# Block transposes on VectorE for maxima and sums over keys, from the seventeenth attention unit on

## The chip, the cores and the metric

One Trainium2 chip, one core. The metric is the device time of one launch in microseconds, the median of the runs. Three runs of the kernel before took 1505.15, 1508.67 and 1516.34 us.

## The reference

Attention with pooled queries, then a feed-forward layer with a maximum over three products. Everything is float32.

```python
q, k, v: (8, 8, 1152, 64)          # batch, heads, sequence, head size
q_pool = q.reshape(B, H, S // 2, 2, D).mean(axis=3)          # 576 queries
scores = (1 / sqrt(64)) * q_pool @ k.T
scores = scores - max(scores, over keys)
attn = exp(scores); attn = attn / (sum(attn, over keys) + 1e-9)
x = (attn @ v) -> (4608, 512)      # tokens x (heads * head size)
h = maximum(maximum(x @ w1, x @ w2), x @ w3)                 # 512 -> 768
out = h @ w_out                                              # 768 -> 512
```

The maximum and the sum run over the 1152 keys of one query. In this kernel scores lie with keys on the partitions and queries along the free axis, so both run across partitions. That is the place of the change.

## The kernel before, in words

**Units.** Two heads (a pair) and half of their queries (288) make one unit of attention. There are 8 batches x 4 pairs x 2 halves = 64 units, `d` = 0 to 63; eight units make a batch. The feed-forward part (FFN) of batch b is offered to the planner when the first unit of batch b + 1 has been laid down; that of the last batch comes at the end.

**One unit.** For each of nine blocks of 128 keys TensorE makes scores `pqk` for both heads (L441, L442; keys and queries are kept as a high and a low part). ScalarE copies them to `s` (L447) and VectorE keeps a running maximum `acc` of 128 partitions x 2 heads x 288 queries (L453, L456). Then the maximum over the partitions, for each head: TensorE turns `acc` in three pieces of 96 queries (`rows`, L489, tile `pmt`), VectorE reduces them (`reduce`, L495, tile `m`), and TensorE turns the result back, repeated over all partitions (`bcast`, L502, tile `pmb`). VectorE subtracts `pmb` from `s` (L517), ScalarE takes exp (L523), GpSimd adds the nine blocks of keys to `ksum` (L536, L538), TensorE multiplies with the values (`pav`, L556), ScalarE copies that to `xr` (L565).

**The sum over keys.** For units 16 to 63 (`early` is false) TensorE multiplies `ksum` by a matrix of ones (`total`, L570), 64 columns wide for each head, so that the sum of every query stands on all partitions of its head; ScalarE adds eps (L574), VectorE takes the reciprocal of 128 x 288 (L577), GpSimd scales `xr` (L580). Units 0 to 15 go another way, which the change leaves alone: sums by one-column products (`columns`, L587), eps and reciprocal on six columns, a spread by TensorE (`spread`, L602).

**The FFN.** `xr` is split into a high and a low part (`xh`, L644; `xl`, L647). TensorE makes `ph` (L788), ScalarE and VectorE evacuate it with the maximum over the three weights (L806, L808), the result is split again (L816, L819), TensorE makes `po` (L844). Its weights are converted once, in the first FFN: 24 pieces, each with four instructions on VectorE (L697, L702, L707, L710); later FFNs fetch the converted weights with DMAs.

**What sets the order.** `arrange` is a list scheduler that runs before the program is built. Each step has its engine, a planned cost, the steps it comes after, and a rank (its unit's number plus a constant from the table `RANK`; the FFN's ranks also grow with their place in it). Whenever a planned engine is free it takes the ready step of lowest rank. The order found is the order in which each engine's instructions are issued; every engine works its list strictly in order. The planned costs, such as `pe(400)` for `rows`, only shape that order.

**PSUM.** `ps_a` and `ps_b` are one buffer each: `pmt`, `pmb` of head 0 live in the first, those of head 1 and the value product of later units in the second. `ps_ff` has two buffers for the FFN's products and the sums.

Of the kernel before, what the change touches and what calls it, by code (L numbers as in the profile page):

```python
# [18 lines left out]
P = 128  # L19
D = 64  # L20
NK = 9
NQ = 576
QH = 288
# [5 lines left out]
EPS = 1e-9  # L29
# [2 lines left out]


RANK = {
    "qk": -95.970825,
    "cp": 3.506714,
    "mx": -112.160269,
    "rows": -148.312644,
    "red": 23.466841,
    "bc": -142.276903,  # L40
    "sub": 99.862451,
    "exp": -189.653089,
    "keys": 148.893694,
    "av": 19.232023,
    "xcopy": -206.02547,
    "psum": 18.355097,
    "eps": -181.047585,
    "inv": 113.796689,
    "xm": -22.916262,
    "load": -43.210932,  # L50
    "prep": 250.679273,
    "move": 65.149737,
    "split": -97.511902,
    "ffn": -47.593054,
    "rate": 0.801853,
    "mm": 67.95383,
    "fetch": -234.19152,
    "evac": -68.37474,
    "hhigh": 38.661498,
    "hlow": -51.844784,  # L60
    "conv": 191.981971,
    "rate0": 3.325971,
    "first_qk": 41.083979,
    "first_cp": -105.959101,
    "first_mx": 56.619279,
    "first_sub": 16.712798,
    "first_exp": 260.515882,
    "first_keys": -71.869651,
    "first_av": -60.410117,
    "first_xcopy": 62.582893,  # L70
    "first_psum": -24.318635,
    "first_inv": -22.423915,
    "first_xm": -3.450351,
    "first_load": -260.256351,
    "first_prep": 57.308365,
    "first_move": -123.943607,
    "first_split": 239.216553,
}
LAG = {
    "act": {"act": 0.06, "pe": 0.27},  # L80
# [5 lines left out]
WINDOW = 4096 / 1200  # L86
BUSY = 3072
EARLY = 16
SPLIT = 8
WARM = 10  # L90
APART = 0
# [110 lines left out]
def pe(n):  # L202
    return ("pe", n * 1e-3)
# [6 lines left out]
def dve(n):  # L210
    return ("dve", 0.065 + n / 960)
# [7 lines left out]
def tile_attention_ffn(  # L219
# [9 lines left out]
    nc = tc.nc  # L229
    B = qT.shape[0]  # L230

    cpool = ctx.enter_context(tc.tile_pool(name="cpool", bufs=1))
# [5 lines left out]
    small = ctx.enter_context(tc.tile_pool(name="small", bufs=2))  # L238
# [5 lines left out]
    ps_ff = ctx.enter_context(tc.tile_pool(name="ps_ff", bufs=2, space=PSUM))  # L244
# [7 lines left out]
    eps = cpool.tile([P, 1], F32, name="eps")  # L252
    nc.vector.memset(eps, EPS)

    wo_hi = cpool.tile([P, 6, DM], F32R, name="wo_hi")
    wo_lo = cpool.tile([P, 6, DM], F32R, name="wo_lo")
# [10 lines left out]
    def step(key, at, engines, fn, after, **kw):  # L267
        return Step(plan, lambda: at + R[key] + (R.get("first_" + key, 0) if at < 8 else 0), engines, fn, after, **kw)
# [26 lines left out]
    qk, av, xout, splits, chain = {}, {}, {}, {}, {}  # L295
# [119 lines left out]


    units = {}
    uses, last, finish, scaled, spreads = [[], []], [None], {}, {}, {}

    def scores(d, n, half):  # L420
        o = units[d] = Job()
# [6 lines left out]
        for kk in range(NK):  # L428
            apart = d < APART and kk % 3 == 2
            for hs in [(0, 1), (1, 2)] if apart else [(0, 2)]:  # L430
# [48 lines left out]
                if not apart:  # L479
                    uses.append([c, x])  # L480

        o.rows, o.subs, o.exps, o.pt, o.pb, o.m = [], [[], []], {}, {}, {}, {}
        pools = (ps_a, ps_b)
        for h in range(2):

            def rows(e, h=h):
                o.pt[h] = pools[h].tile([P, 512], F32, tag="ab"[h], name=f"pmt{d}_{h}")
                for i in range(3):
                    nc.tensor.transpose(  # L489
                        o.pt[h][:96, i * P : (i + 1) * P], o.acc[:, h, 96 * i : 96 * i + 96], ident  # L490
                    )

            def reduce(e, h=h):
                o.m[h] = small.tile([96, 3], F32, tag=f"m{h}", name=f"m{d}_{h}")
                nc.vector.tensor_reduce(  # L495
                    o.m[h], o.pt[h][:96, : 3 * P].rearrange("p (t k) -> p t k", t=3), axis=AX.X, op=ALU.max
                )

            def bcast(e, h=h):
                o.pb[h] = pools[h].tile([P, 512], F32, tag="ab"[h], name=f"pmb{d}_{h}")  # L500
                for i in range(3):
                    nc.tensor.transpose(  # L502
                        o.pb[h][:, 96 * i : 96 * i + 96],
                        o.m[h][:, i : i + 1].broadcast_to([96, P]),
                        ident[:96, :96],
                    )
# [3 lines left out]
            o.rows.append(x)  # L510
            x = step("red", d, [("dve", 0.467)], reduce, [x])
            b = step("bc", d + 0.1 * h, [pe(335)], bcast, [x])
# [31 lines left out]
    def values(d, b, j):  # L544
# [19 lines left out]
        def x_copy(e):  # L564
            nc.scalar.copy(x, o.pav[:, :QH])  # L565

        def total(e):
            o.psm = ps_ff.tile([P, 512], F32, tag="ff", name=f"psum{d}")
            for h in range(2):
                nc.tensor.matmul(o.psm[64 * h : 64 * h + 64, :QH], ones, o.ksum[:, h], start=True, stop=True)  # L570

        def add_eps(e):
            o.rs = small.tile([P, QH], F32, tag="rs", name=f"rs{d}", bufs=1)
            nc.scalar.activation(o.rs, o.psm[:, :QH], AF.Identity, bias=eps)  # L574

        def reciprocal(e):
            nc.vector.reciprocal(o.rs, o.rs)  # L577

        def scale(e):
            vec[e].tensor_tensor(x, x, o.rs, op=ALU.mult)  # L580


        def columns(e):
            o.psm = ps_ff.tile([P, 512], F32, tag="ff", name=f"psum{d}")
# [68 lines left out]

        def rest(ready):

            t = chain[d] = step(
                "av" if ready else "psum",
                d + 0.99,
                [pe(486)],
                total,  # L660
                [o.sums[-1]] + ready,
                cols=1152,
                mode=1,
                take="ff",
            )
# [203 lines left out]
    d = n = 0  # L869
# [56 lines left out]
```

## Time and profile before

| | |
|---|---|
| median of three runs | 1508.67 us |
| profiled execution, span from first to last instruction | 1509.3 us |
| granted TensorE clock, mean | 0.963 |
| TensorE busy with products | 1437.4 us, 95% |
| TensorE busy with weight loads (beside the products) | 1234.1 us, 82% |
| VectorE | 1085.3 us, 72% |
| ScalarE | 912.7 us, 60% |
| GpSimd | 1133.2 us, 75% |
| first running maximum of unit 8 / 16 / 32 / 63 on VectorE | 165.6 / 328.3 / 737.2 / 1384.3 us |

In the tables of the profile PE is TensorE's products, PEld its weight loads, DVE VectorE, ACT ScalarE, POOL GpSimd. A group's row gives its line, engine, operation, output and inputs by the program's names, shapes and count, then busy us and the mean ns of one, then idle time in front of it with what ended it. A row in order of time gives start, length, engine and line, count. A row of the windows gives each engine's busy us in that stretch, the granted clock, the DMA engines' busy share and what they moved. The products of L556, L570 and L587 leave two records each, so four records of L570 are two products.

### The profile page before, as it was taken

The page shows a single profiled execution, that of the slowest core. Times are in us where ns is not written, and L with a number is a line of the kernel's source. Part 1 is how long each engine was busy: PE and PEld are TensorE (multiplying, and loading weights), DVE is VectorE, ACT ScalarE, POOL GpSimd, SP SyncE. Part 2 cuts the span into 40 slices and gives each one's busy share as a digit, 9 for nine tenths or more (in the row PEclk, how much of TensorE's full clock was granted, in tenths as well). Part 3 has the DMA queues.
Part 4 walks back from the last instruction along what each step waited for, and adds up shares of the span by engine and source line. Part 5 has one row for each costly group of instructions (what it writes and reads, how often), then busy time and mean ns, then how long its engine had stood idle before and what let it go on. Part 6 is the DMA issues. An engine that isn't in the chain of part 4 may idle for free.

```text
span 1509.3 us, 28532 instructions
## 1 busy us (share of the span) xinstructions
PE 1437.4 (95%) x10640; PEld 1234.1 (82%) x10640; DVE 1085.3 (72%) x1417; ACT 912.7 (60%) x1508; POOL 1133.2 (75%) x867
## 2 busy tenths in 40 slices
PE   7889898989679999999999999999999999999999
PEld 6566676777448999898988888888888988889899
DVE  4889789999897754676668776877578776877310
ACT  4766666775566644565666665776566665666311
POOL 1899899998988547667978787887888787885610
PEclk7878999999869999999999999999999999999999
DMA  6565455565544554456545654565555664562141
GB/s 185 145 176 157 111 166 155 162 197 174 173 112 116 171 165 159 132 163 178 162 139 166 194 183 110 164 192 152 153 150 157 189 189 122 164 178 84 61 163 64
DMA packets 105273, 231.51 MB, mean 153 GB/s; under 512 B 14384, under 2 KB 80816, under 8 KB 95920
## 3 DMA queue, kind: packets, MB, share of 16 engines
q1 hardware_dynamic: 104560, 229.11, 51.7%
q8 instruction: 85, 1.39, 0.4%
q10 hardware_dynamic: 576, 0.59, 0.2%
q14 instruction: 52, 0.43, 0.1%
HBM read 135.27 MB, written 18.87 MB: 102 GB/s over the span
## 4 chain that ended last, share of the span: by engine, by line
PE 66%; POOL 2%; DVE 2%; DMA 1%; issue 1%; ACT 1%; SPq 0%; ACTq 0%; POOLq 0%; DVEq 0%
PE ph L788 26%; PE pav L556 12%; PE po L844 10%; PE pqk L441 7%; PE pqk L442 7%; PE pmt L489 2%; PE psum L570 2%; PE pmb L502 1%; POOL ksum L538 1%; DMA qq<-qraw 1%; POOL xl L647 0%; DVE acc L456 0%; ACT s L447 0%; DMA kraw<-in_kT_dram 0%; DVE w L702 0%
## 5 line engine op out<-in xcount | busy, mean ns | idle before, releaser
L538 POOL TENSOR_TENSOR ksum<-ksum,s 128x576 f32<-128x576 f32 x448 | 650.5, 1452 | 29.6 <-ACT s L523 6.6
L788 PE MATMUL ph<-xh,w 128*128 128x288 f32 x2304 | 532.1, 300 | 11.1 <-DVE hm L808 10.2
L447 ACT COPY s<-pqk 128x576 f32<-128x576 f32 x576 | 361.3, 638 | 127.1 <-PE pqk L442 116.1
L517 DVE TENSOR_TENSOR s<-s,pmb 128x864 f32<-128x864 f32 x384 | 394.4, 1045 | 37.4 <-PE pmb L502 37.3
L788 PEld LDWEIGHTS ph<-xh,w 128*128 128x128 f32 x2304 | 392.7, 189 | 20.4 <-DVE hm L808 12.3
L441 PE MATMUL pqk<-qq,kc 128*128 128x288 f32 x1152 | 358.1, 326 | 40.0 <-DVE acc L456 30.6
L456 DVE TENSOR_TENSOR acc<-acc,pqk 128x576 f32<-128x576 f32 x448 | 334.8, 747 | 85.0 <-ACT s L447 81.7
L523 ACT ACTIVATE s<-s 128x864 f32<-128x864 f32 x384 | 354.4, 929 | 56.7 <-DVE s L517 53.0
L788 PE MATMUL ph<-xl,w 128*128 128x288 f32 x1152 | 341.2, 296 | 0.0
L442 PE MATMUL pqk<-qq,kc 128*128 128x288 f32 x1152 | 333.9, 304 | 0.0
L556 PE MATMUL pav<-s,v 128*64 128x288 f32 x2304 | 308.4, 422 | 0.0
L441 PEld LDWEIGHTS pqk<-qq,kc 128*128 128x128 f32 x1152 | 226.3, 196 | 74.7 <-DVE acc L456 47.1
L556 PEld LDWEIGHTS pav<-s,v 128*64 128x64 f32 x2304 | 167.4, 142 | 120.3 <-issue 17.0
L442 PEld LDWEIGHTS pqk<-qq,kc 128*128 128x128 f32 x1152 | 228.5, 198 | 0.0
L788 PEld LDWEIGHTS ph<-xl,w 128*128 128x128 f32 x1152 | 218.0, 189 | 0.0
L536 POOL TENSOR_TENSOR ksum<-s 128x576 f32<-128x576 f32 x64 | 91.7, 1433 | 105.0 <-ACT s L523 101.3
L819 POOL TENSOR_TENSOR h_lo<-hm,h_hi 128x288 fp32r<-128x288 f32 x96 | 79.1, 827 | 100.4 <-ACT h_hi L816 100.4
L495 DVE TENSOR_REDUCE m<-pmt 96x3 f32<-96x384 f32 x128 | 69.5, 550 | 108.8 <-PE pmt L489 108.6
L808 DVE TENSOR_TENSOR hm<-hm,ph 128x288 f32<-128x288 f32 x192 | 86.1, 449 | 79.0 <-PE ph L788 77.5
L577 DVE RECIPROCAL rs<-rs 128x288 f32<-128x288 f32 (+1 forms) x64 | 96.3, 1505 | 56.5 <-ACT rs L574 54.7
L337 POOL TENSOR_TENSOR kraw<-kraw 128x1152 fp32r<-128x1152 f32 x31 | 83.0, 2678 | 51.3 <-DMA qraw<-in_qT_dram 25.8
L844 PE MATMUL po<-h_hi,wo_hi 128*128 128x288 f32 x384 | 115.9, 302 | 0.0
(55 smaller groups left out, 1467.8 us busy)
## 6 DMA issues: line engine op xcount, KB each, us to landing
w<-w_split SPq DMA_DIRECT2D x63, 1024.0 KB, 5.2
kc<-kraw SPq DMA_DIRECT2D x384, 96.0 KB, 2.3
qq<-qraw SPq DMA_DIRECT2D x252, 144.0 KB, 2.9
v<-in_vr_dram SPq DMA_DIRECT2D x32, 576.0 KB, 3.8
kraw<-in_kT_dram SPq DMA_DIRECT2D x31, 576.0 KB, 4.6
qraw<-in_qT_dram SPq DMA_DIRECT2D x31, 576.0 KB, 4.3
w<-in_win_dram SPq DMA_DIRECT2D x18, 512.0 KB, 6.1
w_split<-w SPq DMA_DIRECT2D x9, 1024.0 KB, 5.0
```

What stands on the lines that cost most here:

```text
L441: nc.tensor.matmul(ps[:, h - hs[0], :QH], w, qq[:, 0, h], start=True, stop=False)
L442: nc.tensor.matmul(ps[:, h - hs[0], :QH], w, qq[:, 1, h], start=False, stop=True)
L447: nc.scalar.copy(o.s[kk // 3][:, kk % 3, slice(*hs)], o.ps[kk, hs][:, :, :QH])
L456: nc.vector.tensor_tensor(acc, acc, ps, op=ALU.max)
L517: nc.vector.tensor_tensor(s, s, o.pb[h][:, None, :QH].broadcast_to([P, 3, QH]), op=ALU.subtract)
L523: nc.scalar.activation(s, s, AF.Exp, scale=SCALE)
L536: vec[e].tensor_tensor(o.ksum, o.s[0][:, 0], x, op=ALU.add)
L538: vec[e].tensor_tensor(o.ksum, o.ksum, x, op=ALU.add)
L556: nc.tensor.matmul(o.pav[64 * h : 64 * h + 64, :QH], pr.v[:, kk, h], o.s[kk // 3][:, kk % 3, h], start=(kk == 0), stop=(kk == NK - 1),)
L577: nc.vector.reciprocal(o.rs, o.rs)
L788: nc.tensor.matmul(t.ps[:, :QH], w[:, a, kk], xx[:, kk, qs], start=(kk == 0 and i == 0), stop=(kk == 3 and i == 2),)
L844: nc.tensor.matmul(t.ps[:, :QH], ww[:, kk, ms], hh[:, kk, qs], start=(kk == 0 and i == 0), stop=(kk == 5 and i == 2),)
```

## The change

From unit 16 on (`TURN = 16`):

- **Maxima.** VectorE reduces every 32 x 32 block of `acc` over the partitions of that block (`blocks`, L501: a reduction that transposes its input by blocks), which leaves 18 columns, in a tile of 72 columns whose rest is zero. TensorE turns this tile once (`turn`, L511). VectorE takes the maximum over the four groups of partitions (`groups`, L515), copies it three times beside itself (`repeat`, L524), TensorE turns it back (`turn_back`, L530), and VectorE spreads it by two block transposes of a broadcast column (`spread_max`, L540), one for each head, into `pmb`.
- **Sums.** VectorE sums every 32 x 32 block of `ksum` in the same way (`block_sums`, L648). TensorE adds the four groups with a matrix `fold` (`fold_sums`, L660), nine columns for each head instead of 288. VectorE adds eps (L666), takes the reciprocal of nine columns (L669) and spreads it by one block transpose (`spread_sums`, L674). ScalarE's addition of eps is gone.
- **Set-up.** `fold` is made from the identity (L258), two tiles are cleared (L266), `eps` is gone.
- **Order.** All constants of `RANK` are new, and with them the place of every step in each engine's list.

Units 0 to 15 keep their steps. The lines above are those of the changed kernel.

```diff
 RANK = {
-    "qk": -95.970825,
+    "qk": -992.300111,
...
+TURN = 16
+ROWS = 72
+BLOCK = 32
...
+        def blocks(e):
+            nc.vector.tensor_reduce(
+                tp[:, : 2 * QH // BLOCK],
+                o.acc.rearrange("p h (b i) -> p (h b) i", i=BLOCK),
+                axis=AX.X,
+                op=ALU.max,
+                apply_transpose=True,
+            )
+
+        def turn(e):
+            o.pb[0] = pools[0].tile([P, 512], F32, tag="a", name=f"pmb{d}_0")
+            nc.tensor.transpose(o.pb[0][:ROWS, 384:512], tp, ident)
+
+        def groups(e):
+            o.m = small.tile([ROWS, P], F32, tag="m", name=f"m{d}")
+            nc.vector.tensor_reduce(
+                o.m[:, :BLOCK],
+                o.pb[0][:ROWS, 384:512].rearrange("b (g i) -> b i g", i=BLOCK),
+                axis=AX.X,
+                op=ALU.max,
+            )
...
+        def turn_back(e):
+            nc.tensor.transpose(o.pb[0][:, 288 : 288 + ROWS], o.m, ident[:ROWS, :ROWS])
+
+        def spread_max(e, h):
+            if h:
+                o.pb[1] = pools[1].tile([P, 512], F32, tag="b", name=f"pmb{d}_1")
+            n = QH // BLOCK
+            nc.vector.transpose(
+                o.pb[h][:, :QH].rearrange("p (b i) -> p b i", i=BLOCK),
+                o.pb[0][:, 288 + n * h : 288 + n * (h + 1), None].broadcast_to([P, n, BLOCK]),
+            )
...
-            x = step("rows", d + 0.1 * h, [pe(400)], rows, [tops[-1], gone] + (old.subs[h] if old else []))
...
+            if d < TURN:
+                x = step("rows", d + 0.1 * h, [pe(400)], rows, [tops[-1], gone] + (old.subs[h] if old else []))
...
+                    x = step("red", d, [dve(2 * QH)], blocks, [tops[-1]])
+                    x = step("rows", d, [pe(150)], turn, [x] + old.subs[0] + old.spreads)
+                    x = step("red", d, [dve(P)], groups, [x])
+                    x = step("red", d, [("dve", 0.17)], repeat, [x])
+                    turned = step("bc", d, [pe(150)], turn_back, [x])
+                b = step("spread", d + 0.1 * h, [dve(QH)], lambda e, h=h: spread_max(e, h), [turned, gone] + old.subs[h])
...
-            t = chain[d] = step("av" if ready else "psum", d + 0.99, [pe(486)], total, [o.sums[-1]] + ready, ...)
-            e1 = step("eps", d, [("act", 0.395)], add_eps, [t, scaled.get(d - 1)], give="ff")
-            t = step("inv", d, [("dve", 1.87)], reciprocal, [e1])
+            t = chain[d] = step("inv", d, [dve(2 * QH)], block_sums, [o.sums[-1], folded.get(d - 2)])
+            t = folded[d] = step("av" if ready else "psum", d + 0.99, [pe(260)], fold_sums, [t] + ready, ...)
+            t = step("inv", d, [("dve", 0.15)], add_eps9, [t, spreads.get(d - 2)], give="ff")
+            t = step("inv", d, [("dve", 0.18)], reciprocal9, [t])
+            t = spreads[d] = step("inv", d, [dve(QH)], spread_sums, [t, scaled.get(d - 1)])
```

Three places of the order. First TensorE in a late unit, around the value product. Before, the key sum (`psum`, two products) stands ahead of the value product (`pav`), then come transpositions (`pmt`) and broadcasts (`pmb`) among the next unit's score products (`pqk`) and FFN products (`ph`):

```order
L570 MATMUL psum_9883<-ksum_9536,ones 64x288 x2
L556 MATMUL pav_9890<-s_0_9465,v_9183 64x288 x6
L556 MATMUL pav_9890<-s_1_9516,v_9183 64x288 x6
L556 MATMUL pav_9890<-s_2_9579,v_9183 64x288 x6
L489 MATMUL pmt_0_9921<-ident,acc_9760 96x128 x3
L441 MATMUL pqk_0_9927<-qq_0_9611,kc_0_9541 128x288
...
L489 MATMUL pmt_1_9935<-ident,acc_9760 96x128 x3
...
L502 MATMUL pmb_0_9948<-ident,m_0_9933 128x96 x3
...
L502 MATMUL pmb_1_9961<-ident,m_1_9945 128x96 x3
```

Now, at the corresponding place:

```order
L455 MATMUL pqk_1_9652<-qq_0_9390,kc_0_9242 128x288
L511 MATMUL pmb_0_9658<-ident,tops_105 72x128
L660 MATMUL psum_9660<-ks_9541,fold 64x9 x2
L628 MATMUL pav_9665<-s_0_9234,v_8956 64x288 x6
L628 MATMUL pav_9665<-s_1_9292,v_8956 64x288 x6
L628 MATMUL pav_9665<-s_2_9354,v_8956 64x288 x6
L530 MATMUL pmb_0_9658<-ident,m_9663 128x72
L932 MATMUL po_2_0_9647<-h_hi_8007,wo_hi 128x288
```

Twelve transpositions of a unit became one turn (L511) and one turn back (L530), and the key sum has nine columns. In this unit the value product stands between the two turns; in most units it is FFN and score products.

Second VectorE in the same place. Before, from the last running maximum (L456) to the first subtractions (L517):

```order
L456 TENSOR_TENSOR acc_9760<-acc_9760,pqk_8_9877 128x576
L577 RECIPROCAL rs_9910<-rs_9910 128x288
L495 TENSOR_REDUCE m_0_9933<-pmt_0_9921 96x3
L495 TENSOR_REDUCE m_1_9945<-pmt_1_9935 96x3
L517 TENSOR_TENSOR s_0_9725<-s_0_9725,pmb_0_9948 128x3x288
```

Now:

```order
L469 TENSOR_TENSOR acc_9463<-acc_9463,pqk_8_9602 128x576
L501 TENSOR_REDUCE tops_105<-acc_9463 128x18
L515 TENSOR_REDUCE m_9663<-pmb_0_9658 72x32
L524 COPY m_9663<-m_9663 72x96
L666 TENSOR_SCALAR rc_9687<-psum_9660 128x9
L669 RECIPROCAL rc_9687<-rc_9687 128x9
L674 STREAM_TRANSPOSE rs_9690<-rc_9687 128x288
L540 STREAM_TRANSPOSE pmb_0_9658<-pmb_0_9658 128x288
L540 STREAM_TRANSPOSE pmb_1_9711<-pmb_0_9658 128x288
L589 TENSOR_TENSOR s_0_9445<-s_0_9445,pmb_0_9658 128x3x288
```

VectorE has eight instructions between the last maximum and the first subtraction where it had three. The sum's block reduction (L648) stands elsewhere, among the running maxima.

Third TensorE at the start of unit 24 (its first `pqk_0`), with the FFN product that stands ahead of it; in `ph_f_j_c` f counts the six column blocks of the FFN, j the three weights, c the half of the tokens. Before:

```order
L788 MATMUL ph_0_1_0_4916<-xh,w_0_3736 128x288 x2
L788 MATMUL ph_0_1_0_4916<-xl,w_0_3736 128x288
L788 MATMUL ph_0_1_0_4916<-xh,w_0_3736 128x288
L441 MATMUL pqk_0_4933<-qq_0_4701,kc_0_4552 128x288
L442 MATMUL pqk_0_4933<-qq_0_4701,kc_0_4552 128x288
```

Now:

```order
L876 MATMUL ph_4_2_1_5287<-xh,w_7_5070 128x288
L876 MATMUL ph_4_2_1_5287<-xl,w_7_5070 128x288
L876 MATMUL ph_4_2_1_5287<-xh,w_7_5070 128x288
L454 MATMUL pqk_0_5292<-qq_0_5052,kc_0_4940 128x288
L455 MATMUL pqk_0_5292<-qq_0_5052,kc_0_4940 128x288
```

When unit 24 begins, the FFN of the second batch stood in its first column block and now stands in its fifth. Counted over the whole list, the FFN products ahead of units 16, 20 and 24 were 276, 432 and 609 and are 399, 627 and 927, of 4608 in all.

More of the change, by code (lines that the diff above doesn't have):

```diff
@@ L34 @@
 RANK = {
-    "qk": -95.970825,
[L36 to L77, printed above, removed]
+    "qk": -992.300111,
+    "cp": 412.643831,
+    "mx": -1545.58781,
+    "rows": -759.1027,
+    "red": -325.246265,
+    "bc": -393.499534,
+    "sub": 2521.190112,
+    "spread": 51.107148,
+    "exp": -1655.988307,
+    "keys": 270.561796,
+    "av": -222.863284,
+    "xcopy": -2706.766959,
+    "psum": 75.873898,
+    "inv": -402.42614,
+    "xm": -2720.80782,
+    "load": 1943.234015,
+    "prep": -435.679461,
+    "move": 73.350202,
+    "split": 2454.226534,
+    "ffn": -1042.838197,
+    "rate": 227.744589,
+    "mm": 2028.536726,
+    "fetch": -804.9704,
+    "evac": 96.686784,
+    "hhigh": 2166.527179,
+    "hlow": -315.242909,
+    "conv": 505.137841,
+    "rate0": 5.466173,
+    "first_qk": 799.041515,
+    "first_cp": -875.506095,
+    "first_mx": -3464.107417,
+    "first_sub": 1648.535981,
+    "first_exp": 1378.011731,
+    "first_keys": -1207.515197,
+    "first_av": 986.355502,
+    "first_xcopy": -999.302149,
+    "first_psum": -259.061214,
+    "first_inv": 793.255621,
+    "first_xm": 2071.499672,
+    "first_load": 345.70598,
+    "first_prep": -968.961452,
+    "first_move": 286.644876,
+    "first_split": -867.421677,
 }
@@ L251, in tile_attention_ffn @@
     nc.vector.memset(ones, 1.0)
-    eps = cpool.tile([P, 1], F32, name="eps")
-    nc.vector.memset(eps, EPS)
+    fold = cpool.tile([P, D], F32, name="fold")
+    for i in range(D // BLOCK):
+        nc.vector.tensor_reduce(
+            fold[:, BLOCK * i : BLOCK * (i + 1)],
+            ident.rearrange("p (g i) -> p i g", i=BLOCK),
+            axis=AX.X,
+            op=ALU.add,
+        )
+    tops_ = [cpool.tile([P, ROWS], F32, name=f"tops{i}") for i in range(2)]
+    for t in tops_:
+        nc.vector.memset(t, 0.0)
     wo_hi = cpool.tile([P, 6, DM], F32R, name="wo_hi")
@@ L417, in tile_attention_ffn @@
     units = {}
-    uses, last, finish, scaled, spreads = [[], []], [None], {}, {}, {}
+    uses, last, finish, scaled, spreads, folded = [[], []], [None], {}, {}, {}, {}
     def scores(d, n, half):
@@ L480, in scores, with repeat @@
                     uses.append([c, x])
+        o.spreads = []
         o.rows, o.subs, o.exps, o.pt, o.pb, o.m = [], [[], []], {}, {}, {}, {}
         pools = (ps_a, ps_b)
+        tp = tops_[d % 2]
+        def blocks(e):
[11 more added lines that the diff above has]
+            o.m = small.tile([ROWS, P], F32, tag="m", name=f"m{d}")
+            nc.vector.tensor_reduce(
+                o.m[:, :BLOCK],
+                o.pb[0][:ROWS, 384:512].rearrange("b (g i) -> b i g", i=BLOCK),
+                axis=AX.X,
+                op=ALU.max,
+            )
+        def repeat(e):
+            n = P // BLOCK - 1
+            nc.vector.tensor_copy(
+                o.m[:, BLOCK:].rearrange("b (g i) -> b g i", g=n),
+                o.m[:, None, :BLOCK].broadcast_to([ROWS, n, BLOCK]),
+            )
+        def turn_back(e):
+            nc.tensor.transpose(
+                o.pb[0][:, 288 : 288 + ROWS],
+                o.m,
+                ident[:ROWS, :ROWS],
+            )
+        def spread_max(e, h):
[5 more added lines that the diff above has]
+                o.pb[0][:, 288 + n * h : 288 + n * (h + 1), None].broadcast_to([P, n, BLOCK]),
+            )
         for h in range(2):
@@ L565, in x_copy @@
             nc.scalar.copy(x, o.pav[:, :QH])
[L567 to L574, printed above, removed]
         def reciprocal(e):
@@ L580, in scale, with block_sums, fold_sums, add_eps9 @@
             vec[e].tensor_tensor(x, x, o.rs, op=ALU.mult)
+        def block_sums(e):
+            o.ks = small.tile([P, 2 * QH // BLOCK], F32, tag="ks", name=f"ks{d}")
+            nc.vector.tensor_reduce(
+                o.ks,
+                o.ksum.rearrange("p h (b i) -> p (h b) i", i=BLOCK),
+                axis=AX.X,
+                op=ALU.add,
+                apply_transpose=True,
+            )
+        def fold_sums(e):
+            n = QH // BLOCK
+            o.psm = ps_ff.tile([P, 512], F32, tag="ff", name=f"psum{d}")
+            for h in range(2):
+                nc.tensor.matmul(
+                    o.psm[64 * h : 64 * h + 64, :n], fold, o.ks[:, n * h : n * h + n], start=True, stop=True
+                )
+        def add_eps9(e):
+            o.rc = small.tile([P, QH // BLOCK], F32, tag="r9", name=f"rc{d}")
+            nc.vector.tensor_scalar(o.rc, o.psm[:, : QH // BLOCK], EPS, None, op0=ALU.add)
+        def reciprocal9(e):
+            nc.vector.reciprocal(o.rc, o.rc)
+        def spread_sums(e):
+            o.rs = small.tile([P, QH], F32, tag="rs", name=f"rs{d}", bufs=1)
+            n = QH // BLOCK
+            nc.vector.transpose(
+                o.rs.rearrange("p (b i) -> p b i", i=BLOCK), o.rc[:, :, None].broadcast_to([P, n, BLOCK])
+            )
         def columns(e):
@@ L654, in rest @@
         def rest(ready):
[L656 to L665, printed above, removed]
-            e1 = step("eps", d, [("act", 0.395)], add_eps, [t, scaled.get(d - 1)], give="ff")
-            t = step("inv", d, [("dve", 1.87)], reciprocal, [e1])
+            t = chain[d] = step("inv", d, [dve(2 * QH)], block_sums, [o.sums[-1], folded.get(d - 2)])
+            t = folded[d] = step("av" if ready else "psum", d + 0.99, [pe(260)], fold_sums, [t] + ready, cols=100, mode=1, take="ff")
+            t = step("inv", d, [("dve", 0.15)], add_eps9, [t, spreads.get(d - 2)], give="ff")
+            t = step("inv", d, [("dve", 0.18)], reciprocal9, [t])
+            t = spreads[d] = step("inv", d, [dve(QH)], spread_sums, [t, scaled.get(d - 1)])
             m = scaled[d] = step("xm", d, [pool(QH)], scale, [t, c])
```

10 lines of the change are left out of this document (7 added, 3 removed).

## The prediction

> **What bounds the kernel now.** I read the page's busy times first, then the windows by stage, then the order of time on TensorE.
>
> ```profile
> span 1509.3 us, 28532 instructions
> PE 1437.4 (95%) x10640; PEld 1234.1 (82%) x10640; DVE 1085.3 (72%) x1417; ACT 912.7 (60%) x1508; POOL 1133.2 (75%) x867
> ```
>
> 95% is a mean over stages. The windows (busy us and count of PE, PEld, DVE, ACT, POOL, then granted clock, DMA share, GB/s) split it:
>
> ```profile
> 0.00:328.00 328.00, 288.68 (x2021) 224.91 (x2021) 271.49 (x375) 212.65 (x329) 270.15 (x193) 0.90 0.58 161
> 250.00:400.00 150.00, 127.90 (x951) 105.96 (x951) 139.11 (x181) 96.99 (x158) 138.16 (x101) 0.95 0.59 174
> 400.00:450.00 50.00, 39.03 (x189) 25.03 (x190) 48.06 (x52) 28.90 (x44) 44.77 (x31) 0.70 0.44 123
> 737.00:905.00 168.00, 167.59 (x1287) 146.96 (x1287) 125.06 (x162) 110.82 (x186) 134.50 (x106) 1.00 0.55 163
> 905.00:1072.00 167.00, 166.35 (x1278) 145.72 (x1277) 123.82 (x160) 110.32 (x184) 133.30 (x104) 1.00 0.57 164
> 1420.00:1510.00 90.00, 86.03 (x647) 84.08 (x642) 13.28 (x26) 16.14 (x39) 13.31 (x17) 1.00 0.29 101
> ```
>
> There are two regimes. Up to 450 us VectorE and GpSimd are the busy ones (DVE 139.11 of 150, then 48.06 of 50), TensorE has gaps and its granted clock sinks to 0.70. From there on TensorE is busy 99.7% of the time at clock 1.00, and VectorE has a quarter of the time free (125.06 of 168). Where the units stand is seen from the first running maximum of units 16, 24, 40 and 48 on VectorE:
>
> ```profile
> 328.27 0.74 DVE L453 TENSOR_TENSOR acc<-s,pqk 128x576 f32<-128x576 f32 x1
> 520.89 0.74 DVE L453 TENSOR_TENSOR acc<-s,pqk 128x576 f32<-128x576 f32 x1
> 904.55 0.76 DVE L453 TENSOR_TENSOR acc<-s,pqk 128x576 f32<-128x576 f32 x1
> 1072.12 0.76 DVE L453 TENSOR_TENSOR acc<-s,pqk 128x576 f32<-128x576 f32 x1
> ```
>
> A steady batch of eight units takes 1072.12 - 904.55 = 167.6 us, 20.9 us a unit, all of it TensorE. The change touches the 48 units from index 16 on, nearly all of them in the TensorE regime.
>
> Busy time alone could mislead, so I checked the starts. In order of time on TensorE (start, length, line, count):
>
> ```profile
> 916.10 0.30 PE L844 MATMUL po<-h_hi,wo_lo 128*128 128x288 f32 x1
> 916.24 0.49 PE L489 MATMUL pmt<-ident,acc 128*96 128x128 f32 x3
> 916.48 0.38 PE L441 MATMUL pqk<-qq,kc 128*128 128x288 f32 x1
> 916.70 0.29 PE L442 MATMUL pqk<-qq,kc 128*128 128x288 f32 x1
> ...
> 917.75 0.29 PE L844 MATMUL po<-h_hi,wo_lo 128*128 128x288 f32 x1
> 917.88 0.41 PE L502 MATMUL pmb<-ident,m 96*128 96x96 f32 x3
> 918.08 0.38 PE L844 MATMUL po<-h_hi,wo_hi 128*128 128x288 f32 x1
> 918.30 0.29 PE L844 MATMUL po<-h_lo,wo_hi 128*128 128x288 f32 x1
> 918.42 0.30 PE L844 MATMUL po<-h_hi,wo_lo 128*128 128x288 f32 x1
> ```
>
> Lengths overlap; the price of work is the distance between starts, 0.13 us for a 288-column product (918.30 to 918.42).
>
> The Trainium skill (Perfetto Trace Analysis, section Identifying the Most-Contended Engine) speaks against trusting the 99.7%: it says that pipelined matmuls make busy time a poor measure and tells one to take the weight loads' busy share. Here that is 146.96 of 168, 87%; if only that share of the removed time came back, the 59 us found below would be 51 and the forecast 1437. I go by the starts, which follow each other at 0.13 us without a hole.
>
> **What the change takes from TensorE.** Between 916.10 and 916.70 two ordinary steps would take 0.27 us, so three row transpositions cost 0.33 us; between 917.75 and 918.30 three broadcasts cost 0.28 us. Each stands twice in a unit: 0.66 + 0.56. The old key sum (L570):
>
> ```profile
> 467.98 0.71 PE L570 MATMUL psum<-ksum,ones 128*64 128x288 f32 x4
> 468.51 4.54 PE L556 MATMUL pav<-s,v 128*64 128x288 f32 x36
> ```
>
> takes 0.53 us beside the value product. Removed: 1.75 us a unit.
>
> Added: one transposition of 128 columns, 0.33 / 3 = 0.11 us; one back of 72 columns, 0.28 / 3 = 0.09 us; two narrow sums of nine columns. No row shows these; the nearest are the one-column sums of the early units:
>
> ```profile
> 287.07 0.29 PE L442 MATMUL pqk<-qq,kc 128*128 128x288 f32 x1
> 287.20 1.10 PE L587 MATMUL psum<-ones,ksum 128*96 128x1 f32 x12
> 288.16 0.38 PE L441 MATMUL pqk<-qq,kc 128*128 128x288 f32 x1
> ```
>
> Twelve records in 288.16 - 287.20 = 0.96 us, 0.08 us each; the two new sums should leave four records like L570's: 0.32 us. Added: 0.52 us. Saved: 1.23 us a unit, x48 = **59 us**. Bounds: if a single transposition costs as much as a group of three and the narrow sum as much as the old one (0.33 + 0.28 + 0.53 = 1.14), 0.61 us a unit or 29 us; if the narrow sum is free, 1.55 us or 74 us. I take 59, since every row shows a price per record.
>
> **What it adds to VectorE.** Rows of the groups of instructions by line (count, busy us, mean ns of one):
>
> ```profile
> L456 DVE TENSOR_TENSOR acc<-acc,pqk 128x576 f32<-128x576 f32 x295 | 220.9, 749 | 64.5 <-ACT s L447 61.9
> L577 DVE RECIPROCAL rs<-rs 128x288 f32<-128x288 f32 x43 | 83.7, 1947 | 42.5 <-ACT rs L574 40.8 <-POOL ksum L538 1.6
> L808 DVE TENSOR_TENSOR hm<-hm,ph 128x288 f32<-128x288 f32 x139 | 62.3, 448 | 25.3 <-PE ph L788 23.9
> L495 DVE TENSOR_REDUCE m<-pmt 96x3 f32<-96x384 f32 x85 | 46.8, 552 | 97.1 <-PE pmt L489 97.1
> ```
>
> 576 and 288 elements take 749 and 448 ns: 1.04 ns an element and 0.15 us fixed; the reduction of 384 lies on the same line (552). The reciprocal costs (1947 - 150) / 288 = 6.2 ns an element. By the first price the two block reductions over 576 elements take 0.75 us each, the group maximum (128) 0.28, the copy (96) 0.25, the three block transposes (288) 0.45 each, the addition of eps 0.16, the reciprocal of nine 0.21: 3.75 us. Gone are two reductions (1.10) and the wide reciprocal (1.95): 3.05 us. VectorE gains 0.70 us a unit, 34 us in all, ScalarE loses its addition of eps. Per steady unit VectorE goes from 125.06 / 8 = 15.6 to 16.3 us, and TensorE from 20.9 to 19.7 us: still 17% free, so this I cost at nothing. It is hidden under TensorE's own work, and if that cover went, the 34 us would be paid.
>
> Whether an element of a block transpose costs 1.04 ns is shown by no row. Bounds: nothing per element, and the reciprocal's 6.2 ns (2016 elements a unit: 10.4 us more). I take the reductions' price, the nearest kind of operation. The Trainium skill (Vector Engine (DVE) Microarchitecture Reference, section The reshape front-end and per-opcode configuration) says that the transposing front end sustains one element per cycle per lane; by it too the block operations cost what I take, and no run yet shows it.
>
> The maxima's chain grows: block reduction, turn, group maximum, copy, turn back, two transposes, where it was transposition, reduction, broadcast. TensorE's turn and turn back stand in its queue ahead of FFN products, so a late VectorE would stop TensorE. In the new order the value product (4.5 us) stands between turn and turn back in 8 units and ten or more products (1.3 us) in the other 40, against 0.28 + 0.25 us on VectorE, so I cost this at nothing too; without that cover it would be about half a microsecond a unit, 25 us.
>
> **What the new order moves.** Counted in the two orders, FFN products ahead of unit 24's first score product are 609 before and 927 now, 318 more, at 0.13 us: 42 us of TensorE work drawn forward out of the saturated regime. It pays only as far as TensorE has holes to take it. Of 521 us up to unit 24, TensorE idles 328 - 288.68 = 39 us before unit 16 and 50 - 39.03 = 11 us between 400 and 450. But the engine in front there is VectorE, and all weight conversions now end within unit 16 instead of unit 20; one conversion on VectorE is the sum of
>
> ```profile
> L702 DVE SCALAR_TENSOR_TENSOR w<-w_m,w 128x512 uint32<-128x512 uint32 x24 | 34.2, 1424 | 0.3
> L710 DVE SCALAR_TENSOR_TENSOR w<-w,w_m 128x512 f32<-128x512 uint32 x24 | 33.0, 1374 | 0.4
> L707 DVE TENSOR_SCALAR w_m<-w 128x512 uint32<-128x512 uint32 x24 | 24.9, 1038 | 0.3
> L697 DVE TENSOR_SCALAR w<-w_m 128x512 uint32<-128x512 uint32 x24 | 22.0, 917 | 7.5 <-ACT w_m L694 3.2 <-issue 2.9 <-POOL xr L580 0.9
> ```
>
> 4.75 us, and some six of them move ahead of unit 16, so unit 16 comes up to 28 us later. Ends: 0 us if that eats the gain, 42 us if none of it is lost. I take half, **21 us**.
>
> **Sum.** 1509.3 - 59 - 21 = 1429 us against the profiled execution's span; the runs' median of 1508.67 is 0.6 us from it, so the same holds for the median. The forecast's own range is 1509 - 74 - 42 = 1393 to 1509 - 29 = 1480.
>
> **Rivals.** (a) *Slower: VectorE becomes the bound through the block operations.* Place: from unit 16 (328 us) to the tail at 1420. VectorE's work there is 1085.3 - 271.5 - 13.3 = 800 us, with the change 834. The share it kept up over a long window was 139.11 / 150 = 0.93. At three times the price (3.1 ns an element) a unit gains 4.2 us: (834 + 202) / 0.93 = 1114 us, and with 328 and 90 around it **1531 us**. It turns slower from 2.8 times on (1092 x 0.93 = 1016 = 834 + 48 x 3.8). For it: the reciprocal shows that one instruction can be six times off the usual price. Against: all other rows of VectorE lie on one line. Chance 0.06.
> (b) *TensorE waits at turn and turn back.* One late handover of 1.23 us a unit eats the whole saving and leaves the order's part: **1488 us**. For it: VectorE is fed in a fixed order, and the group maximum stands behind whatever is ahead of it. Against: from 450 to 1380 us TensorE stood idle for only 2.0 us in front of the score products, where VectorE's running maximum would hold it:
>
> ```profile
> L441 PE MATMUL pqk<-qq,kc 128*128 128x288 f32 x758 | 220.6, 306 | 2.0 <-ACT s L447 1.2 <-DVE acc L456 0.3 <-DVE acc L453 0.2
> ```
>
> Chance 0.10.
> (c) *The new order costs the first stage.* Unit 16 comes 28 us later, none of it made up, and only the 399 - 276 = 123 FFN products already done by then (16 us) come back: 1509 - 59 + 28 - 16 = **1462 us**. For it: VectorE at 0.93 and 0.96 there. Against: TensorE has holes there too. Chance 0.10.
> That the change does nothing because TensorE isn't the limit is held by the starts at 0.13 us to be near nil.
>
> **How the numbers follow.** The forecast 1429 has 0.74, (a) 0.06, (b) 0.10, (c) 0.10. The range 1395 to 1485 holds (c) and nearly all of the forecast's own and leaves out (a), most of (b) and the extreme ends. A measurement of this kernel can tell about 1%, or 15 us, from no change. Faster by more: the forecast, (c) and four tenths of (b), 0.88. Within 1%: the rest of (b), 0.06. Slower: (a), 0.06.
>
> **What would show it.** TensorE busy above 99% at clock 1.00 from unit 20 on, a steady batch near 167.6 - 8 x 1.23 = 158 us, the transposing reductions near 0.75 us and the block transposes near 0.45 us, no wait of TensorE for the group maximum in the first rows of the waits, and unit 24 beginning near 532 us with 318 more products behind it (520.89, plus the half of 42 us that is not won, less the saving of eight units). A steady batch still near 167 us, with TensorE waiting for VectorE, would make it wrong by (a) or (b); a unit 24 at 565 us or later by (c).

## The result, and the profile after

The changed kernel takes 1432.87 us (median of four runs, 1432.28 to 1433.66) against 1509.22 us of the kernel before: ratio 0.9491, 95% interval 0.9464 to 0.9518. 1429 was forecast. The profiled execution spans 1430.6 us.

```profile
span 1430.6 us, 27636 instructions
PE 1358.5 (95%) x10160; PEld 1180.7 (83%) x10160; DVE 1094.2 (76%) x1708; ACT 901.9 (63%) x1460; POOL 1125.5 (79%) x867
```

TensorE's busy time fell by 78.9 us and the span by 78.7 us; the time in which TensorE is idle (span less busy time) is 72.1 us where it was 71.9. VectorE's busy time rose by 8.9 us. TensorE's share stayed at 95%: the kernel is bound as before, with less to do. The windows of the changed kernel, with the columns of before:

```profile
0.00:328.00 328.00, 280.84 (x1933) 221.14 (x1934) 266.48 (x369) 202.70 (x312) 256.91 (x186) 0.90 0.57 163
250.00:400.00 150.00, 117.17 (x810) 94.82 (x806) 140.57 (x180) 89.36 (x143) 137.88 (x98) 0.87 0.55 163
400.00:450.00 50.00, 49.13 (x363) 44.28 (x364) 32.95 (x51) 29.93 (x50) 34.13 (x25) 0.93 0.43 115
855.00:1010.00 155.00, 155.00 (x1199) 137.56 (x1198) 126.39 (x209) 108.72 (x177) 132.81 (x104) 1.00 0.63 176
```

Between 250 and 400 us TensorE is worse off than it was (117.17 busy instead of 127.90, clock 0.87 instead of 0.95), between 400 and 450 much better (49.13 instead of 39.03, clock 0.93 instead of 0.70): the last weight conversion on VectorE ends at 393.6 us instead of 454.0. In a steady batch TensorE is busy without any hole, 155.00 of 155. The first running maxima of units 16, 24, 40 and 48 show what a batch takes:

```profile
360.29 0.74 DVE L466 TENSOR_TENSOR acc<-s,pqk 128x576 f32<-128x576 f32 x1
543.60 0.75 DVE L466 TENSOR_TENSOR acc<-s,pqk 128x576 f32<-128x576 f32 x1
854.54 0.75 DVE L466 TENSOR_TENSOR acc<-s,pqk 128x576 f32<-128x576 f32 x1
1009.94 0.75 DVE L466 TENSOR_TENSOR acc<-s,pqk 128x576 f32<-128x576 f32 x1
```

1009.94 - 854.54 = 155.4 us, where it was 167.6: 1.52 us a unit less. Unit 16 begins 32 us later than before, unit 24 is 22.7 us later, but with 318 more FFN products behind it.

The new work on TensorE, in order of time (start, length, line, count):

```profile
863.40 0.29 PE L455 MATMUL pqk<-qq,kc 128*128 128x288 f32 x1
863.62 0.29 PE L660 MATMUL psum<-ks,fold 128*64 128x9 f32 x4
863.76 4.57 PE L628 MATMUL pav<-s,v 128*64 128x288 f32 x36
...
869.28 0.29 PE L455 MATMUL pqk<-qq,kc 128*128 128x288 f32 x1
869.41 0.27 PE L511 MATMUL pmb<-ident,tops 128*72 128x128 f32 x1
869.44 0.38 PE L932 MATMUL po<-h_hi,wo_hi 128*128 128x288 f32 x1
869.65 0.29 PE L932 MATMUL po<-h_lo,wo_hi 128*128 128x288 f32 x1
...
870.73 0.30 PE L932 MATMUL po<-h_hi,wo_lo 128*128 128x288 f32 x1
870.86 0.23 PE L530 MATMUL pmb<-ident,m 72*128 72x72 f32 x1
870.89 0.38 PE L932 MATMUL po<-h_hi,wo_hi 128*128 128x288 f32 x1
871.11 0.29 PE L932 MATMUL po<-h_lo,wo_hi 128*128 128x288 f32 x1
```

Read by the distance of starts, less 0.27 us for two ordinary steps: the turn costs 0.37 - 0.27 = 0.10 us, the turn back 0.38 - 0.27 = 0.11 us, the narrow sums 863.76 - 863.62 = 0.14 us. Note the lengths, 0.27 and 0.23 us: they would have doubled the price. The new work on VectorE, groups by line from 450 to 1300 us:

```profile
L540 DVE STREAM_TRANSPOSE pmb<-pmb 128x288 f32<-128x288 f32 x87 | 43.2, 497 | 33.1 <-PE pmb L530 28.6 <-ACT xr L637 2.9
L648 DVE TRANSPOSE_TENSOR_REDUCE ks<-ksum 128x18 f32<-128x576 f32 x44 | 33.7, 766 | 2.2 <-POOL ksum L610 2.1
L501 DVE TRANSPOSE_TENSOR_REDUCE tops<-acc 128x18 f32<-128x576 f32 x44 | 33.7, 766 | 0.2
L674 DVE STREAM_TRANSPOSE rs<-rc 128x288 f32<-128x288 f32 x44 | 20.9, 475 | 1.5
L515 DVE TENSOR_REDUCE m<-pmb 72x32 f32<-72x128 f32 x44 | 12.4, 283 | 81.2 <-PE pmb L511 81.2
L524 DVE COPY m<-m 72x96 f32<-72x96 f32 x44 | 10.8, 246 | 1.3
```

With the 150 ns that the prediction takes as fixed, an element costs (766 - 150) / 576 = 1.07 ns in the block reductions and (475 - 150) / 288 = 1.13 or (497 - 150) / 288 = 1.20 ns in the block transposes: near the 1.04 ns of the other operations and far from the reciprocal's 6.2 ns. The Trainium skill (Vector Engine (DVE) Microarchitecture Reference, section The reshape front-end and per-opcode configuration) says that the transposing front end sustains one element per cycle and lane. The trace agrees in so far as the transposing instructions cost little more per element than the others.

### The profile page after: what moved, and what is told of

Read it like the earlier page. It is cut to its first block, busy times and chain, and to the rows that moved or that the text cites. A ratio compares the mean times of both kernels' runs of the same rounds, so it can differ in the third digit from the quotient of the medians.

```text
span 1430.6 us, 27636 instructions
## 1 busy us (share of the span) xinstructions
PE 1358.5 (95%) x10160; PEld 1180.7 (83%) x10160; DVE 1094.2 (76%) x1708; ACT 901.9 (63%) x1460; POOL 1125.5 (79%) x867
## 4 chain that ended last, share of the span: by engine, by line
PE 76%; POOL 7%; DVE 5%; DMA 4%; issue 4%; ACT 2%; SPq 1%; ACTq 0%; POOLq 0%; DVEq 0%
PE ph L876 28%; PE pav L628 17%; PE po L932 10%; PE pqk L454 10%; PE pqk L455 9%; POOL ksum L610 3%; DVE acc L469 2%; DMA qraw<-in_qT_dram 1%; DMA qq<-qraw 1%; SPq L384 1%; DMA kraw<-in_kT_dram 1%; DVE w_m L795 1%; DMA w<-in_wout_dram 1%; DMA w<-in_win_dram 1%; PE psum L660 1%
## 5 line engine op out<-in xcount | busy, mean ns | idle before, releaser
L589 DVE TENSOR_TENSOR s<-s,pmb 128x864 f32<-128x864 f32 x384 | 394.0, 1042 | 1.3 <-PE pmb L563 0.7
L454 PE MATMUL pqk<-qq,kc 128*128 128x288 f32 x1152 | 347.1, 316 | 35.1 <-DVE acc L469 26.3
L455 PE MATMUL pqk<-qq,kc 128*128 128x288 f32 x1152 | 330.8, 302 | 0.0
L454 PEld LDWEIGHTS pqk<-qq,kc 128*128 128x128 f32 x1152 | 223.6, 194 | 72.4 <-DVE acc L469 37.7
L628 PEld LDWEIGHTS pav<-s,v 128*64 128x64 f32 x2304 | 165.6, 142 | 116.7 <-issue 17.2
L455 PEld LDWEIGHTS pqk<-qq,kc 128*128 128x128 f32 x1152 | 225.0, 195 | 0.0
L932 PE MATMUL po<-h_hi,wo_lo 128*128 128x288 f32 x384 | 113.7, 296 | 0.0
L932 PE MATMUL po<-h_lo,wo_hi 128*128 128x288 f32 x384 | 113.7, 296 | 0.0
```

The costliest lines, as they stand in the source:

```text
L454: nc.tensor.matmul(ps[:, h - hs[0], :QH], w, qq[:, 0, h], start=True, stop=False)
L455: nc.tensor.matmul(ps[:, h - hs[0], :QH], w, qq[:, 1, h], start=False, stop=True)
L589: nc.vector.tensor_tensor(s, s, o.pb[h][:, None, :QH].broadcast_to([P, 3, QH]), op=ALU.subtract)
L628: nc.tensor.matmul(o.pav[64 * h : 64 * h + 64, :QH], pr.v[:, kk, h], o.s[kk // 3][:, kk % 3, h], start=(kk == 0), stop=(kk == NK - 1),)
L932: nc.tensor.matmul(t.ps[:, :QH], ww[:, kk, ms], hh[:, kk, qs], start=(kk == 0 and i == 0), stop=(kk == 5 and i == 2),)
```

## The experiments

Theory 1: TensorE's records are the price, and the order must only leave TensorE without holes. Its rivals: the new order brings most of the gain; the wide reciprocal on VectorE did; TensorE has slack. Times of several sessions are compared through their ratio to the kernel before.

### One half of the change at a time

Sums alone (the first diff, against the changed kernel) and maxima alone (the second, cut), both with the new constants:

```diff
-TURN = 16
+TURN = 64
```

```diff
-            t = chain[d] = step("inv", d, [dve(2 * QH)], block_sums, ...)
...
+            t = chain[d] = step("av" if ready else "psum", d + 0.99, [pe(486)], total, ...)
+            e1 = step("eps", d, [("act", 0.395)], add_eps, ...)
+            t = step("inv", d, [("dve", 1.87)], reciprocal, [e1])
```

> Only the sums over keys go the new way; the maxima of all units keep transposition, reduction and broadcast, under the new constants of the order. Theory 1 (TensorE's records are the price: a unit saves about 0.42 us by the narrow sum and 1.08 us by the turns, the order gives some 7 us): 48 x 0.42 + 7 = 27 us, so about 1482 us. Theory 2 (the new order brings most of the gain): about 1445 us, close to the full change. Theory 3 (the wide reciprocal on VectorE was what held the kernel, 1.95 us a unit): most of the gain, about 1445 us too, but then with few waits of the scaling for the reciprocal.

Measured: 1508.83 us, ratio 0.9992 (0.9977 to 1.0007).

> Only the maxima go the new way; the sums keep the wide product with ones, eps on ScalarE and the wide reciprocal, under the new constants. Theory 1: 48 x 1.08 + 7 = 59 us, about 1450 us, a steady batch near 167.6 - 8.6 = 159 us. Theory 2: about 1445 us. Theory 3: about 1500 us, since the wide reciprocal stays.

Measured: 1476.52 us, ratio 0.9776 (0.9757 to 0.9796).

Both miss theory 1, by 27 and 26 us, and theory 2 by more. Theory 3 falls too: with the wide reciprocal gone the sums alone gain nothing, and the maxima alone, which keep it, gain 33 us where theory 3 gave 9. The page of the sums alone:

```profile
span 1507.8 us, 28451 instructions
PE 1423.2 (94%) x10640; PEld 1231.4 (82%) x10640; DVE 1045.9 (69%) x1564; ACT 893.2 (59%) x1460; POOL 1129.9 (75%) x867
```

TensorE's busy time fell by 14.2 us, but its idle time rose from 71.9 to 84.6 us. With the maxima alone it fell by 50.3 us (to 1387.1), and the idle time rose to 88.3 us; a batch took 160 to 166 us where 159 was expected. So both halves took work off TensorE, and part of it came back as waiting. Either the halves need each other, or the constants of the order, which were chosen for the full change, don't suit a half. The next two runs ask that.

### Steps and constants exchanged

New steps with the constants of before (the diff, cut, against the changed kernel), and old steps with the new constants (the same exchange in the kernel before):

```diff
 RANK = {
-    "qk": -992.300111,
+    "qk": -95.970825,
...
+    "spread": -142.276903,
```

> All steps of the change, but the order made with the constants of before (the new step of spreading the maxima takes the old broadcast's constant). Theory 1: the steady batch stays at 155 us and only the order's part of the gain goes, about 1440 us. Theory 2: the order's gain goes, 1480 us or more. The rival that TensorE waits at the turns unless the order was made for them: steady batch above 160 us and 1470 us or more.

Measured: 1486.24 us, ratio 0.9842 (0.9822 to 0.9863).

> The kernel before, all steps as they were, with the order made by the new constants (eps on ScalarE takes the constant of the reciprocal). Theory 1: the order is worth some 7 us, about 1502 us, and not far from no change, since the constants were not chosen for these steps. Theory 2 (the new order brings most of the gain): 1460 us or less.

Measured: 1523.49 us, ratio 1.0082 (1.0053 to 1.0112).

The new constants make the old steps slower, and the old constants leave the new steps 53 us behind the changed kernel. With the old steps TensorE is busy for 1437.4 us, as in the kernel before, and idle for 12.5 us more (1521.8 - 1437.4 = 84.4 us). So the new order is not a gain by itself; it is one that fits the new steps. What a misfit looks like, new steps with old constants, a steady batch of 162 us (window, then TensorE's longest waits in it: us in total, times, longest; the lines are those of that run's kernel, one higher than in the changed kernel):

```profile
892.00:1054.00 162.00, 155.47 (x1160) 133.52 (x1159) 126.87 (x208) 106.40 (x175) 131.55 (x103) 0.98 0.56 167
```

```profile
PE pqk L455 <- DVE acc L470: 3.4, 4, 1.0
PE psum L661 <- DVE ks L649: 1.1, 1, 1.1
PE pqk L455 <- DVE acc L467: 0.7, 1, 0.7
```

6.5 us of holes in a batch, mostly in front of score products that wait for a running maximum to free their PSUM buffer. Theory 1 missed by 46 us. The rival was right in time and batch, but only partly in place: 0.3 us of the waits are at the turn itself, 1.1 us at the narrow sum. The expected 155 us a batch needs the order.

### The same order, more work on TensorE

These kernels keep every instruction in the changed kernel's place and repeat some of them, to no effect on the result.

```diff
-            nc.tensor.transpose(o.pb[0][:ROWS, 384:512], tp, ident)
+            for _ in range(5):
+                nc.tensor.transpose(o.pb[0][:ROWS, 384:512], tp, ident)
```

> The changed kernel, but the turn of the block maxima is made five times into the same place, four times for nothing: 4 x 0.109 us on TensorE a unit, with nothing added elsewhere and the planner not told. Theory 1: 48 x 0.44 = 21 us, about 1454 us. If TensorE had slack (its 99.9% busy only an effect of overlapping records): near 1433 us.

Measured: 1448.79 us, ratio 0.9593 (0.9569 to 0.9617); by ratio 15 us above the changed kernel, a steady batch 158.4 us.

```diff
             for h in range(2):
+                nc.tensor.matmul(o.psm[64 * h : 64 * h + 64, 32 : 32 + QH], ones, o.ksum[:, h], start=True, stop=True)
```

> The changed kernel in exactly its order, with the old wide products of ones and the key sums made once more beside the narrow ones, into columns that nobody reads. If, in an order without holes, TensorE's records are the price: 0.53 us a unit, 48 x 0.53 = 25 us, about 1458 us. If the order as such made the gain: near 1433 us.

Measured: 1452.97 us, ratio 0.9615 (0.9583 to 0.9647); 19 us above.

The wide sum as in that run, and `turn` and `turn_back` six times each (cut, line breaks left out):

```diff
+            for _ in range(6):
+                nc.tensor.transpose(o.pb[0][:ROWS, 384:512], tp, ident)
...
+            for _ in range(6):
+                nc.tensor.transpose(o.pb[0][:, 288 : 288 + ROWS], o.m, ident[:ROWS, :ROWS])
```

> The same, and the turn and the turn back made six times each, so that TensorE carries about the old load (12 transpositions and the wide sum) in the new order, while VectorE and ScalarE do the new work: 5 x 0.097 + 5 x 0.07 + 0.53 = 1.36 us a unit more, 65 us, about 1498 us, if the records are the price. If the order made the gain: 1460 us or less.

Measured: 1493.45 us, ratio 0.9889 (0.9865 to 0.9913); by ratio (0.9889 - 0.9491) x 1510 = 60 us above. Its steady batch:

```profile
881.00:1047.00 166.00, 166.00 (x1317) 147.34 (x1316) 127.07 (x210) 110.02 (x177) 133.98 (x105) 1.00 0.59 165
```

VectorE, ScalarE and GpSimd do what they do in the changed kernel, TensorE has no hole, and the batch takes 165.6 us again. With TensorE's records given back, 60 of 77 us are gone, so they were most of the gain. The other 17 us are what the new order, and what the new steps spare the other engines, bring together under about the old load of TensorE; no run tells these two apart.

The three runs cost 15, 19 and 60 us where 21, 25 and 65 were expected. In a steady batch the added instructions take 3.5, 3.9 and 10.7 us by the distances of starts, and the batch grew by 3.0, 3.4 and 10.2 us (from 155.4 to 158.4, 158.9 and 165.6): some half a microsecond less each time, whatever was added.

### The same order, more work on VectorE

0.77 us a unit more in two places: the block maximum twice, on the chain that TensorE's turn waits for, and the block sum twice, beside it.

```diff
         def blocks(e):
-            nc.vector.tensor_reduce(tp[:, : 2 * QH // BLOCK], ...)
+            for _ in range(2):
+                nc.vector.tensor_reduce(tp[:, : 2 * QH // BLOCK], ...)
```

```diff
         def block_sums(e):
-            nc.vector.tensor_reduce(o.ks, ...)
+            for _ in range(2):
+                nc.vector.tensor_reduce(o.ks, ...)
```

> The changed kernel with the block maximum made twice in each late unit, so 0.77 us more on VectorE (37 us in all), in the chain that TensorE's turn waits for, unknown to the planner. If VectorE's free time covers it and the turn has room: within 5 us of the changed kernel, about 1435 us. If TensorE waits for the chain: up to 37 us, about 1470 us, with waits of TensorE's turn for the block maximum.

Measured: 1439.64 us, ratio 0.9534 (0.9509 to 0.9558); 6 us above the changed kernel.

> The changed kernel with the block sum made twice in each late unit: the same 0.77 us more on VectorE, but beside the chain of the maxima. If only the load of VectorE counts, the same as with the block maximum twice. If the chain counts: nearer to the changed kernel than that one, about 1434 us.

Measured: 1466.27 us, ratio 0.9712 (0.9673 to 0.9751); 33 us above.

I had it the wrong way round: the place on the chain is the cheap one. A steady batch of each, block maximum twice first, with TensorE's waits:

```profile
859.00:1016.00 157.00, 155.45 (x1199) 137.19 (x1198) 132.13 (x216) 108.98 (x176) 132.91 (x105) 1.00 0.62 174
```

```profile
PE pmb L512 <- DVE tops L502: 1.6, 4, 0.4
```

The waits make 1.6 of the 2.1 us by which a batch grew (157.5 against 155.4). Then the block sum twice:

```profile
869.00:1030.00 161.00, 157.38 (x1204) 138.43 (x1203) 132.89 (x217) 109.74 (x177) 133.41 (x105) 1.00 0.61 170
```

```profile
PE pqk L454 <- DVE acc L469: 3.1, 7, 0.5
PE pqk L454 <- DVE m L524: 0.5, 1, 0.5
```

VectorE's busy time is the same within 1 us (132.13 and 132.89), far from full in both. The block sum stands in VectorE's list among the running maxima; twice as long it holds up the next maximum, which holds a PSUM buffer that the next score product needs. One place, VectorE and then TensorE in order of time:

```profile
869.85 0.72 DVE L469 TENSOR_TENSOR acc<-acc,pqk 128x576 f32<-128x576 f32 x1
870.49 1.58 DVE L649 TRANSPOSE_TENSOR_REDUCE ks<-ksum 128x18 f32<-128x576 f32 x2
871.99 0.41 DVE L897 TENSOR_TENSOR hm<-hm,ph 128x288 f32<-128x288 f32 x1
872.32 0.74 DVE L469 TENSOR_TENSOR acc<-acc,pqk 128x576 f32<-128x576 f32 x1
873.12 0.40 PE L454 MATMUL pqk<-qq,kc 128*128 128x288 f32 x1 [0.49 <-DVE acc L469]
```

The running maximum behind the two block sums ends at 873.06, and the score product starts at 873.12 after 0.49 us of idle time. The waits shown make 3.6 of the 5.3 us by which a batch grew (160.7 against 155.4). The block maximum comes after the last running maximum of its unit, and the turn behind it has some room.

The same with the double cost told to the planner:

```diff
-            t = chain[d] = step("inv", d, [dve(2 * QH)], block_sums, ...)
+            t = chain[d] = step("inv", d, [("dve", 2 * (0.065 + 2 * QH / 960))], block_sums, ...)
```

> The block sum made twice as in the earlier run, but the planner is told its double cost and makes the order anew with the same constants. If VectorE's load is the trouble: about 1466 us again. If only the place in the order was: about 1436 us. If any order that the constants were not chosen for has holes: 1450 to 1470 us, with the holes spread over other waits than those for the running maximum.

Measured: 1467.85 us, ratio 0.9728 (0.9694 to 0.9762).

```profile
PE pqk L454 <- DVE acc L469: 1.8, 1, 1.8
PE pqk L454 <- ACT s L460: 1.6, 1, 1.6
PE pmb L530 <- DVE m L524: 1.4, 1, 1.4
PE pqk L454 <- PE pqk L455: 0.5, 1, 0.5
```

The time alone can't tell the first reading (VectorE's load) from the third. The block maximum twice, with the same load and 27 us less, speaks against the load, and the waits of a steady batch (871 to 1037 us) are spread over the running maximum, ScalarE's copy and the chain of the maxima, as the third reading had it.

### In all units

```diff
-EARLY = 16
-TURN = 16
+EARLY = 0
+TURN = 0
...
```

> The new way of maxima and sums in all 64 units, with the changed kernel's constants. In units 0 to 15 VectorE is ahead: it gains about 1.9 us a unit there, 30 us, while TensorE has holes and its saving of some 2 us a unit is worth little. If VectorE bounds that stage: about 1455 us, unit 16 some 25 us later. If TensorE's price counted there as well: 1405 us.

Measured: 1497.36 us, ratio 0.992 (0.9893 to 0.9946). Unit 16 begins at 369.9 us, only 10 us later than in the changed kernel; but the batches from unit 24 on take 161 to 169 us, though their steps and constants are those of the changed kernel. Another beginning gave the planner another order for all that follows. In the first 250 us TensorE is busy for 202.96 us at a granted clock of 0.81, where the changed kernel has 215.68 us at 0.89. The run says little on the early units; it says again how much hangs on the order.

### The sums alone, with an order that fits

The constants were searched for these steps, starting from those of before.

```diff
 RANK = {
...
-TURN = 16
+TURN = 64
```

> The sums alone go the new way, as in the first run, but with constants that were searched for these steps, starting from those of before. If the narrow sum's 0.4 us of TensorE a unit is worth its price once the order fits: 48 x 0.4 = 19 us and somewhat more where VectorE is relieved early, about 1488 us, a steady batch near 164 us with TensorE without holes. If the narrow sum is worth nothing without the turns: 1505 us or more, as in the first run.

Measured: 1487.61 us, ratio 0.9828 (0.9783 to 0.9872), against 0.9992 with the unfitting constants. The batches from unit 24 on take 163.2 to 164.7 us; one of them, and the page:

```profile
870.00:1033.00 163.00, 161.99 (x1274) 144.28 (x1274) 119.56 (x184) 107.10 (x175) 132.31 (x104) 1.00 0.59 168
```

```profile
span 1485.3 us, 28504 instructions
PE 1413.6 (95%) x10640; PEld 1229.7 (83%) x10640; DVE 1049.4 (71%) x1564; ACT 899.2 (61%) x1460; POOL 1129.4 (76%) x867
```

TensorE's holes are down to 1.0 us of this batch, and its idle time is 71.7 us of the whole run, as in the kernel before, where the first run had 84.6. So the first run's failure was the order's: the narrow sum has its price on its own. That price is 48 x (0.53 - 0.14) = 19 us; the run gained 26. No run searched the constants anew for the old steps, nor for the maxima alone, so what the search by itself brings is not shown.

## Why the prediction was right, point by point

**The bound.** Right: TensorE without holes after 450 us, and time follows its records (three kernels with repeated work in the same order). The reading by the weight loads' share (the Trainium skill, Perfetto Trace Analysis, section Identifying the Most-Contended Engine), 1437 us, lies as near to the result as the forecast. The run with the old load tells a little more: by the distances of starts in its steady batches it adds 0.49 us of sums, 0.54 us of turns and 0.31 us of turns back to a unit, 8 x 1.34 = 10.7 us to a batch, and the batch rose by 10.2 us, 95% of it. That does not decide against the 87%: with the turn made five times the batch rose by 3.0 of 3.5 us (85%), with the wide sum beside the narrow one by 3.4 of 3.9 us (88%). About half a microsecond is missing in each of the three, so the full price less a small fixed slack in a batch fits them better than a share.

**What TensorE saves.** 1.23 us a unit were forecast. The turn came out as said (0.10 for 0.11), the turn back at 0.11 for 0.09, and the narrow sums at 0.14 instead of 0.32: a record of nine columns with 64 columns of weights takes less than half of the one-column, 96-column record that I priced it by. That makes 1.40 us, 67 us in all instead of 59. The batch gained 1.52 us a unit. Of the other 0.12, the idle time that TensorE had before (1.06 us in the two batches of the prediction's windows) makes 0.07; the rest is not traced to its place.

**What VectorE pays.** 2 x 0.77 + 0.28 + 0.25 + 2 x 0.50 + 0.48 + 0.16 + 0.19 = 3.9 us a unit for the forecast's 3.75. The taken price of a block transpose was nearly right (0.45 us for 0.48 and 0.50), so rival (a) fell. But these are lengths, and where VectorE works without a pause its records overlap too: in the steady batch a subtraction starts at 853.57 us, takes 1.06 us and so ends 0.09 us after the running maximum behind it has started, at 854.54. Its busy time rose only from 15.5 us a unit (123.82 of 167 us) to 15.8 (126.39 of 155), by 0.3 us where 0.70 was forecast. The added work cost nothing, but not for the reason given. I had costed it at nothing because VectorE had 17% of its time free. The block sum made twice had as much free time above it and cost 33 us. The step came out right and its ground is wrong: cover is the room at that place in the list, not a share of the engine's time.

**Rival (b).** TensorE has no wait at turn or turn back in the steady batches of the changed kernel. It has one before them: the first turn, at 383 us, waits 6.9 us for VectorE's subtraction (L589). The 6 us of the block maximum made twice show that there is less than 0.77 us of room there.

**The order's part.** Mis-sized: 21 us forecast, some 11.5 us left of the 78.7 us when 67.2 us of records are taken off; the old-load run, which splits it another way, gives 17. Unit 24 began at 543.6 us and not at 532: unit 16 came 32 us later, as rival (c) had it, but units 16 to 24 made up 9 us while doing more FFN work. By these starts 543.6 - 520.9 + 8 x 1.40 = 34 us of the 42 us drawn forward were paid before unit 24 (an estimate, since it takes the steady saving for these units), so 8 us were won where 21 were forecast. That the order could be a term of its own, added to the steps', is what the runs refuse: alone it is 12 us slower on the old steps, and without it the new steps lose 53 us. The sum held because both kernels compared have an order that fits.

**The total** was right within 4 us partly by luck. By the distances of starts two errors, 8 us too little for TensorE and 9.5 us too much for the order, nearly cancelled; by the old-load run's split (60 and 17 us) they are 1 and 4 us.

## What to carry to other kernels

Where one engine has no holes, price an edit by the distance between starts of its instructions, not by their lengths: this gave 65 us for the old load, where 60 were measured. Before an edit is judged in a kernel whose order was searched, search the order again for it; the same edit measured 0 us with a foreign table and 26 us with its own. And free time of an engine covers new work only where the work stands: ask which buffer the next instruction in that engine's list sets free.

## What the runs showed that I had not expected

- The same 0.77 us on VectorE, with the order unchanged, cost 6 us in one place and 33 us in another.
- TensorE's idle time over the whole run was 71.9, 72.1 and 71.7 us in the kernel before, the changed kernel and the sums alone with their own constants, though the first two are 78.7 us apart. In the two halves and the two exchanges, whose constants were chosen for other steps, it was 84 to 98 us.
- Four records of a nine-column product beside the value product take 0.14 us; the twelve one-column records of the early units take 0.08 us each. The number of weight columns (64 and 96) differs and so does the neighbour; which of the two makes the difference no run tells.
- A block transpose from PSUM to PSUM (497 ns) costs 22 ns more than one from SBUF to SBUF (475 ns) for the same 288 elements.
